# Attention and two MLPs on one core: the second head pair's transposes ahead of the first scores, a longer landing time for the gate rows in the planner, and shifted tile starts for the first MLP

## The chip, the core and the metric

The kernel runs on one core of a Trainium2 chip. Its engines are TensorE (PE; PEld is its weight load), VectorE (DVE), ScalarE (ACT), GpSimd (POOL) and SyncE (SP), which here only issues DMAs; a few DMAs are issued by ACT. The metric is the device time of one execution in microseconds. Before the change the median of three runs is 842.57 us (842.36 to 842.8). What can be told from no change here is about 0.2%, that is 1.7 us.

## The reference

For 4 batches of 8 heads (576 positions, 64 columns a head) a causal attention with a gate bias:

```python
scores = scale * np.matmul(q, k.transpose(0, 1, 3, 2))
cum = np.cumsum(np.maximum(s, 0.0), axis=-1)
scores = where(causal, -1e9, scores + min(-(cum_i - cum_j), 0))
attn = exp(scores - max) / (sum + 1e-9);  x = attn @ v
```

Then, on the 2304 tokens of 512 columns, a first MLP (512 to 1024 and back), `h = x @ w_in`, `solu = h * softmax(h)`, a layer norm with `g_ln`, `@ w_out`, and a second MLP (512 to 2048 and back) with `g = h * clip(h + 3, 0, 6) / 6`.

## The kernel before

**Two halves of an operand.** Where full precision is wanted, an operand is split into a high and a low part, and each product is three matmuls (high by high, low by high, high by low) that add up in one PSUM bank. L813 is the first product of the first MLP (weights loaded from `xh`/`xl`, `w_in_h`/`w_in_l` streamed, 128x512), L900 its second (weights loaded from `w_out`, `zh`/`zl` streamed, 128x256), L1072 and L1103 are those of the second MLP. `w_out` lies in two tiles a half: the first five chunks in one, the last `LATE_OUT` = 3 in another, which serves as score buffer first.

**Attention.** Heads go in pairs. For the first four pairs (`prep_whole`, L432) q and k are turned by PE in two groups of three transposes each (L441), and copied by ACT (q, L446) and DVE (k, L448). A score tile (`qk_whole`, L554; matmuls L584) adds two products: the gate rows (tile `whole`, rows 2 and 3) and q by k (tile `HL`, or rows 0 and 1 of `whole` from the third pair on). DVE masks and takes the row maximum (L532), ACT takes the exponential (L544), DVE the reciprocal of the row sums (L640), POOL scales (L645), PE transposes the result (L679), and L708 multiplies by v.

**Gate rows.** `gate_rows` (L266) loads `s`, sums it up on DVE, splits it (L279 to L283) and stores rows to DRAM (`rows_d`, L287); `load_gates` (L424, L428) loads each pair's rows from there into `whole`.

**The order of the work** is not that of the code. Every step is handed to a planner with an engine, a cost and the steps that it depends on; `lag` is the time that the planner allows for a DMA's landing after its issue, and `after` makes a step wait until another has begun. The planner plays the steps through with these costs, and each engine gets its instructions in that order; on the chip each engine then runs its own list from the top, waiting at each instruction until its inputs are there. The SP queue issues DMAs in the same way. So a changed cost or dependency can reorder all engines, up to where the plan comes back to the old one.

**Where tiles start.** Pools lay tiles one behind the other in each partition, so a tile's start follows from the sizes before it. Counted from a multiple of 512 bytes (128 floats, the row of one weight load), the starts are, as worked out from the pools:

| tile | L | before | with the change |
|---|---|---|---|
| xh, xl (weights) | 813 | 320 | 448 |
| w_in_h, w_in_l (streamed) | 813 | 448 | 448 |
| w_out, first five chunks (weights) | 900 | 448 | 480 |
| w_out, last three chunks (weights) | 900 | 480 | 480 |
| zh, zl (streamed) | 900 | 448 | 448 |
| x2h, x2l, w2, gh, gl | 1072, 1103 | 480 | 480 |

The tiles of the attention (`ap1`, `ap2`: whole, HL, raw q and k, y, pt, V) start 128 bytes later with the change; the second MLP's stay.

Of the kernel before, what the change touches and what calls it, by code (L numbers as in the profile page):

```python
# [10 lines left out]
F32 = mybir.dt.float32  # L11
# [177 lines left out]
def kernel(ctx, tc, q, k, v, s, w_in, w_out, g_ln, w2_in, w2_out, out):  # L189
# [5 lines left out]
    P = 128  # L195
    NH = B * H
    NPAIR = H // 2
# [38 lines left out]
    def w_out_part(late):  # L236
        for x in "hl":
            w_out_t[x, late] = w1p.tile([P, LATE_OUT if late else KFF - LATE_OUT, DM], F32R, tag=f"w_out_{x}{late:d}", name=f"w_out_{x}{late:d}")

    def w_out_at(x, c):  # L240
        late = c >= KFF - LATE_OUT
        return w_out_t[x, late][:, c - (KFF - LATE_OUT) * late, :]

    w_out_part(False)
    g_sb = w1p.tile([P, KFF], F32, name="g_sb")


    at = ExitStack()
# [6 lines left out]
        return banks[plan.bank[key]]  # L255


    mask = ap1.tile([P, 480 + P], F32, name="mask")
    nc.gpsimd.memset(mask, 0.0)
    nc.gpsimd.affine_select(out=mask[:, 480:], in_=mask[:, 480:], pattern=[[-1, P]], compare_op=ALU.is_ge, fill=NEG, base=0, channel_multiplier=1)  # L260
# [5 lines left out]
    def gate_rows():  # L266


        s_sb = ap2.tile([P, S], F32, tag="y4", name="s_sb")[:NH]
        one = ap2.tile([P, S], F32, tag="y4", name="one")[:NH]  # L270
        cum = ap2.tile([P, NQ, 2, D], F32, tag="V", name="cum").rearrange("p c j d -> p (c j d)")[:NH, :S]
        pos = ap2.tile([P, PT_COLS], F32, tag="pt", name="pos", bufs=PT).bitcast(F32R)[:NH, : 2 * S]
        neg = ap2.tile([P, PT_COLS], F32, tag="pt", name="neg", bufs=PT).bitcast(F32R)[:NH, : 2 * S]

        def load():
            nc.sync.dma_start(out=s_sb, in_=s.rearrange("b h s -> (b h) s"))

        def sums():
            nc.vector.tensor_scalar_max(s_sb, s_sb, 0.0)  # L279
            nc.vector.tensor_tensor_scan(cum, one, s_sb, 0.0, ALU.mult, ALU.add)  # L280
            nc.vector.tensor_copy(pos[:, :S], cum)
            nc.vector.tensor_sub(pos[:, S:], cum, pos[:, :S].bitcast(F32))
            nc.vector.tensor_scalar_mul(neg, pos.bitcast(F32), -1.0)  # L283

        def put(i, r, src):
            dst = rows_d[:, i, r::2, :]
            nc.sync.dma_start(out=dst, in_=src)  # L287

        def zeros(j):
            whole_t[j] = ap1.tile([P, 4, S], F32, tag=f"stack{j}", name=f"whole{j}")  # L290
            nc.gpsimd.memset(whole_t[j][:, 2:4, :], 0.0)

        plan.add("SP", 0.45, load, writes=["s"], lag=2.0)
        plan.add("POOL", 2.2, lambda: nc.gpsimd.memset(one, 1.0), writes=["one"])
        plan.add("DVE", 3.0, sums, reads=["s", "one"], writes=["c"])
        ones = one.unsqueeze(1).to_broadcast([NH, 2, S])
        both = lambda c: c.bitcast(F32).rearrange("p (i s) -> p i s", i=2)
        for i, r, src, key in ((1, 0, both(pos), "c"), (0, 1, both(neg), "c"), (0, 0, ones, "one"), (1, 1, ones, "one")):
            plan.add("SP", 0.55, lambda i=i, r=r, src=src: put(i, r, src), reads=[key], writes=[f"rows/{i}{r}"], lag=2.0)
        for j in range(2):  # L300
            plan.add("POOL", 1.3, lambda j=j: zeros(j), writes=[f"zeros{j}"], new=[(f"stack{j}", 1, f"whole{j}")])

# [251 lines left out]
    def qk_whole(p, t):  # L554

        n, w = SZ[t], ST[t] + SZ[t]
        heads = (2 * p, 2 * p + 1)
        late = ST[t] >= CUT
        ts = [i for i in range(NQ) if (ST[i] >= CUT) == late]

        def homes():
            for h, x in zip(heads, "hl"):
                if p % 2 == 0:
                    ys[h, t] = ap2.tile([P, w], F32, tag=f"y{t}", name=f"y{h}_{t}")
                elif t == ts[0]:
                    cols = sum(ST[i] + SZ[i] for i in ts)
                    if late:
                        y = w1p.tile([P, LATE_OUT, DM], F32, tag=f"w_out_{x}1", name=f"yl{h}").rearrange("p c n -> p (c n)")
                    else:
                        y = ap2.tile([P, cols], F32, tag="y2", name=f"yf{h}")  # L570
                    o = 0
                    for i in ts:
                        ys[h, i] = y[:, o : o + ST[i] + SZ[i]]
                        o += ST[i] + SZ[i]

        def mm(c0, c1, keys):
            if c0 == 0:
                homes()
            for m in range(2):
                for j in range(2):  # L580
                    r = slice(j * D, (j + 1) * D)
                    g, hl = gates_at(p, j), hls[f"HL{p}"][r]
                    a, b = (hl[:, 0, :], hl[:, 1, :]) if m else (g[:, 0, :], g[:, 1, :])
                    nc.tensor.matmul(bank(keys[j])[:n, : c1 - c0], lhsT=a[:, ST[t] : w], rhs=b[:, c0:c1], start=(m == 0), stop=(m == 1))  # L584

        pieces = pieces_of(t)
        for c0, c1, at in pieces:
            keys = [f"sc{h}_{t}_{c0}" for h in heads]
            new = []
            if c0 == 0 and p % 2 == 0:  # L590
                new = [(f"y{t}", 2, f"y{h}_{t}") for h in heads]
            elif c0 == 0 and t == ts[0]:
                new = [("wlate", 1, f"yl{p}")] if late else [("y2", 2, f"yf{h}") for h in heads]
            plan.add("PE", 4 * max(0.07, 0.00033 * (c1 - c0)), lambda c0=c0, c1=c1, keys=keys: mm(c0, c1, keys),
                     reads=[f"HL{p}/{x}{c}" for x in "qk" for c in ((0, 3) if late else (0,))] + [f"G{p}{late:d}", f"whole{p % 2}"], writes=keys, new=new, bank=keys, after=[f"sc{heads[0]}_{t}_0"] if c0 else [])
            for h, key in zip(heads, keys):
                plan.add("DVE", dve(c1 - c0), lambda h=h, c0=c0, c1=c1, at=at, key=key: tops(h, t, c0, c1, at, key), reads=[key],
                         writes=[f"{y_key(h, t)}/{c0}", f"nmax{h}_{at}"])
        for h in heads:
            exps(h, t, pieces)  # L600
# [146 lines left out]
    def pairs(a):  # L747

        r = []
        ts = [t for t in range(NQ) if (ST[t] >= CUT) == a]  # L750
        for p in range(NPAIR):
            last = (p - 1, a) if p else (NPAIR - 1, 0) if a else None
            step = [] if last is None else [(0.0, lambda last=last: norm_part((2 * last[0], 2 * last[0] + 1), bool(last[1])))]
            turns = [] if last is None else [(0.4, lambda h=h, gi=gi: tr(h, gi)) for gi in ((1, 2, 3) if last[1] else (0,)) for h in (2 * last[0], 2 * last[0] + 1)]
            extra = []
            if not a:
                if p + 1 < NPAIR:
                    extra = [(0.3, lambda p=p: prep_qk(p + 1, "q")), (0.3, lambda p=p: prep_qk(p + 1, "k"))]
                extra += [(0.0, lambda p=p: load_qk(p + 2))] if p + 2 <= NPAIR else []
                extra += [(0.0, lambda p=p: load_v(p + 1, 0))] if p + 1 < NPAIR else [(0.0, lambda: load_v(0)), (0.0, lambda: load_gates(0, 1))]  # L760
            elif p + 1 < NPAIR:
                extra = [(0.0, lambda p=p: load_gates(p + 1, 1)), (0.0, lambda p=p: load_v(p + 1))]
                if p == NPAIR - 2:
                    extra += [(0.5, lambda: prep_qk(NPAIR, "q")), (0.5, lambda: prep_qk(NPAIR, "k")), (0.0, lambda: load_qk(NPAIR + 1))]
            else:
                extra = [(0.0, lambda: load_v(NPAIR))]
            qs = [(0.0013 * (ST[t] + SZ[t]), lambda p=p, t=t: qk_whole(p, t)) for t in ts]
            k = 0
            for i, x in enumerate(qs):
                step.append(x)  # L770
                for rest in (turns, extra):
                    n = -(-len(rest) * (i + 1) // len(qs)) - -(-len(rest) * i // len(qs))
                    at = -(-len(rest) * i // len(qs))
                    step.extend(rest[at : at + n])
            if last is not None:
                step.append((1.0, lambda last=last: av(last[0], (last[1],))))
            r.append(step)
        return r
# [26 lines left out]
    def ffn1_h(i, f, kk):  # L805
        key = f"h{i}_{f}"

        def mm():
            if f == kk == 0:
                sts[i] = bcp.tile([P, 16], F32, tag="st", name=f"st{i}")  # L810
                es[i] = bcp.tile([P, 2, 512], F32, tag="e", name=f"e{i}")
            for m in range(3):
                nc.tensor.matmul(bank(key), lhsT=xs[i][m // 2][:, kk, :], rhs=(w_in_l if m == 1 else w_in_h)[:, kk, f * 512 : (f + 1) * 512],  # L813
# [162 lines left out]
    for name in "qk":  # L976
        prep_qk(0, name)
    load_qk(1)
    load_v(0, 0)
    plan.add("SP", 0.5, lambda: nc.sync.dma_start(out=g_sb, in_=g_ln.rearrange("(c p) -> p c", p=P)), writes=["g"], lag=2.0, after=["HL0/k0"])  # L980
    for b, share in enumerate(SHARES):
# [212 lines left out]
```

## Time and profile before

| | before |
|---|---|
| median of 3 runs | 842.57 us |
| the profiled execution | 840.6 us, of it 838.8 us span |
| PE busy | 810.9 us, 97% of the span |
| PEld busy | 686.1 us, 82% |
| DVE, ACT, POOL busy | 52%, 48%, 25% |
| DMA | 77.52 MB, mean 92 GB/s |

The page's first part gives busy time by engine. Views of the trace give the same by stretch (the windows), instructions in order of time (the timeline, with idle time and what ended it in brackets), groups of equal instructions (by line and form), and the chain of work that ended last. A matmul's duration runs from its start to its modelled end, and the next one starts well before that end; so a duration is compared with that of another matmul of the same shape, not added up.

### The profile page before, as it was taken

Reading aid. Unit: us, or ns where it says so; the run is one execution under the profiler, and the core shown is the slowest. Engines: PE = TensorE matmul, PEld = TensorE weight load, DVE = VectorE, ACT = ScalarE, POOL = GpSimd, SP = SyncE. Lnnn points to the kernel's source line nnn. Section 1 sums busy time; section 2 is a strip of 40 time slices with the busy share of each in tenths; the row PEclk is TensorE's granted clock in tenths of the full one; section 3 lists DMA queues with packets and bytes.
Section 4 is the critical chain, followed back from the end, with each engine's and each line's share of the span. In section 5 each row is a group of like instructions: output and inputs, shape, how many; then the busy total and the mean of one; then the engine's idle time right before and its main releaser. Section 6 shows DMA issues by size and latency. Waiting matters only on the chain.

```text
span 838.8 us, 13546 instructions
## 1 busy us (share of the span) xinstructions
PE 810.9 (97%) x4864; PEld 686.1 (82%) x4864; DVE 438.5 (52%) x1125; ACT 399.4 (48%) x928; POOL 209.9 (25%) x309
## 2 busy tenths in 40 slices
PE   3889999999999999999999999999999999999997
PEld 2555688898898889888999999998888888888886
DVE  3787887746855674739826992233222232222221
ACT  2575767755765575736635762244222322232222
POOL 2564644424632364327412220000000000000000
PEclk9999999999999999999999999999999999999999
DMA  6753596855656465323615640012000300010001
GB/s 163 194 150 112 126 214 148 175 121 125 130 119 137 99 130 121 65 95 117 198 38 192 215 152 1 0 63 89 1 0 1 101 1 0 1 51 1 0 1 50
DMA packets 95938, 77.52 MB, mean 92 GB/s; under 512 B 64288, under 2 KB 78112, under 8 KB 95872
## 3 DMA queue, kind: packets, MB, share of 16 engines
q1 hardware_dynamic: 93568, 68.27, 32.7%
q10 hardware_dynamic: 2304, 8.39, 3.0%
q8 instruction: 38, 0.62, 0.3%
q14 instruction: 28, 0.23, 0.1%
HBM read 45.38 MB, written 10.03 MB: 66 GB/s over the span
## 4 chain that ended last, share of the span: by engine, by line
PE 91%; DVE 4%; POOL 2%; DMA 2%; issue 1%; ACT 1%; POOLq 0%; DVEq 0%; SPq 0%; ACTq 0%
PE bank L1072 24%; PE bank L1103 23%; PE bank L900 11%; PE bank L813 10%; PE bank L708 6%; PE bank L679 5%; PE bank L611 5%; PE bank L584 3%; PE bank L879 2%; PE bank L474 1%; POOL y L645 1%; DVE y L532 1%; DMA stack<-HL12k 1%; DMA rows_d<-neg 1%; POOL y L627 0%
## 5 line engine op out<-in xcount | busy, mean ns | idle before, releaser
L1072 PE MATMUL bank<-x2h,w 128*128 128x512 f32 (+1 forms) x640 | 183.7, 368 | 0.0
L1103 PE MATMUL bank<-w,gh 128*128 128x512 f32 x576 | 177.0, 390 | 0.0
L1080 DVE SCALAR_TENSOR_TENSOR g<-g,bank 128x512 f32<-128x512 f32 (+1 forms) x80 | 50.7, 633 | 204.4 <-ACT g L1076 204.1
L1072 PEld LDWEIGHTS bank<-x2h,w 128*128 128x128 f32 x640 | 118.8, 188 | 17.5
L1076 ACT ACTIVATE g<-bank 128x512 f32<-128x512 f32 (+1 forms) x80 | 44.5, 556 | 178.2 <-PE bank L1072 177.9
L1103 PEld LDWEIGHTS bank<-w,gh 128*128 128x128 f32 x576 | 107.7, 188 | 21.0
L1072 PE MATMUL bank<-x2l,w 128*128 128x512 f32 (+1 forms) x320 | 117.8, 368 | 0.0
L1103 PE MATMUL bank<-w,gl 128*128 128x512 f32 x288 | 111.8, 391 | 0.0
L532 DVE CUSTOM_DVE_ANT_0 y<-bank,mask 96x288 f32<-96x288 f32 (+4 forms) x168 | 74.7, 467 | 57.4 <-PE bank L611 38.0
L544 ACT ACTIVATE y<-y,nmax 128x256 f32<-128x256 f32 (+4 forms) x140 | 83.4, 598 | 39.8 <-DVE nmax L532 27.5
L627 POOL TENSOR_SCALAR y<-y,rsum 128x128 f32<-128x128 f32 (+4 forms) x120 | 68.6, 590 | 103.8 <-DVE rsum L623 45.2
L900 PE MATMUL bank<-zh,w_out_h 128*128 128x256 f32 x288 | 82.8, 287 | 0.0
L900 PE MATMUL bank<-zl,w_out_h 128*128 128x256 f32 x288 | 81.2, 282 | 0.0
L900 PE MATMUL bank<-zh,w_out_l 128*128 128x256 f32 x288 | 81.2, 282 | 0.0
L1088 DVE TENSOR_TENSOR gl<-g,gh 128x512 fp32r<-128x512 f32 (+1 forms) x80 | 51.8, 647 | 42.2 <-ACT gh L1084 41.9
L1084 ACT CAST gh<-g 128x512 fp32r<-128x512 f32 (+1 forms) x80 | 46.2, 578 | 47.4 <-DVE g L1080 47.3
L1072 PEld LDWEIGHTS bank<-x2l,w 128*128 128x128 f32 x320 | 60.1, 188 | 7.5
L1103 PEld LDWEIGHTS bank<-w,gl 128*128 128x128 f32 x288 | 54.0, 188 | 11.3
L813 PE MATMUL bank<-w_in_h,xh 128*128 128x512 f32 x144 | 60.9, 423 | 0.8 <-DVE xh L795 0.8
L611 PE MATMUL bank<-stack 128*96 128x288 f32 (+4 forms) x288 | 57.8, 317 | 0.8 <-DMA stack<-HL12k 0.8
L813 PE MATMUL bank<-w_in_h,xl 128*128 128x512 f32 x144 | 56.9, 395 | 0.6 <-POOL xl L799 0.6
L813 PE MATMUL bank<-w_in_l,xh 128*128 128x512 f32 x144 | 56.8, 394 | 0.0
(220 smaller groups left out, 1356.4 us busy)
## 6 DMA issues: line engine op xcount, KB each, us to landing
raw_w2i<-in_moe_w_in_dram SPq DMA_DIRECT2D x16, 512.0 KB
raw_w2o<-in_moe_w_out_dram SPq DMA_DIRECT2D x16, 512.0 KB
rawq<-in_q_dram SPq DMA_DIRECT2D x32, 144.0 KB
rawk<-in_k_dram SPq DMA_DIRECT2D x32, 144.0 KB
x_d<-x2s SPq DMA_DIRECT2D x36, 128.0 KB
out_dram<-ob SPq DMA_DIRECT2D x18, 256.0 KB
raw_wi<-in_moe_w_in_dram ACTq DMA_DIRECT2D x8, 512.0 KB
raw_wo<-in_moe_w_out_dram ACTq DMA_DIRECT2D x8, 512.0 KB
```

What stands on the lines that cost most here:

```text
L532: nc.vector.tensor_tensor_reduce(out=ys[h, t][:n, c0:c1], in0=bank(key)[:n, : c1 - c0], in1=mask[:n, 480 + n - w + c0 : 480 + n - w + c1], ...
L544: nc.scalar.activation(out=y[:n], in_=y[:n], func=AF.Exp, bias=nmax[:n, h, t : t + 1], scale=-1.0, accum_out=sums[:n, h, t : t + 1])
L611: nc.tensor.matmul(bank(key)[:n, : c1 - c0], lhsT=ss[:, 2 - 2 * m, ST[t] : w], rhs=ss[:, 3 - 2 * m, c0:c1], start=(m == 0), stop=(m == 1))
L627: nc.gpsimd.tensor_scalar(ys[h, t][:n], ys[h, t][:n], rsum[:n, h, t : t + 1], 1.0, ALU.mult, ALU.mult)
L708: nc.tensor.matmul(bank(key)[j * D : (j + 1) * D, lo - c0 : c1 - c0], lhsT=vs[v_key(p, a)][:n, jj, j, :], rhs=pts[pt_key(2 * p + j, a)][:n ...
L813: nc.tensor.matmul(bank(key), lhsT=xs[i][m // 2][:, kk, :], rhs=(w_in_l if m == 1 else w_in_h)[:, kk, f * 512 : (f + 1) * 512], start=(kk ...
L900: nc.tensor.matmul(bank(key)[:, : 2 * P], lhsT=w_out_at(w, kk)[:, m * P : (m + 1) * P], rhs=z[:, kk, :], start=(kk == 0 and i == 0), stop= ...
L1072: nc.tensor.matmul(bank(key)[:, :w], lhsT=wt[:, a, 0, c * P : (c + 1) * P], rhs=x[:, c, :w], start=(c == 0 and i == 0), stop=(c == KDM - 1 ...
L1080: nc.vector.scalar_tensor_tensor(out=gg, in0=gg, scalar=6.0, in1=bank(key)[:, :w], op0=ALU.min, op1=ALU.mult)
L1084: nc.scalar.copy(gh[:, :w], gg[:, :w])
L1088: nc.vector.tensor_sub(gl[:, :w], gg[:, :w], gh[:, :w].bitcast(F32))
L1103: nc.tensor.matmul(bank(key), lhsT=g_t[ci, m][1 + i // 2][:, t * P : (t + 1) * P], rhs=w2[m][:, i % 2, 1, :], start=(m == 0 and i == 0), s ...
```

## The change

There are five edits. The turns of q and k of the second pair (`prep_qk(1, ...)`) are handed to the planner right behind the loads of that pair, and no longer among the extras of the first pair's scores; the first pair's first scores get an `after` on the last of these turns (`pp1k3`). The planner's `lag` for the stores of the gate rows goes from 2.0 to 4.5. `g_sb` (32 bytes a partition) is laid in front of the first `w_out` tiles instead of behind them; `st` of the first MLP grows from 16 to 64 floats; a tile of 32 floats that nothing uses (`apart_too`) stands in front of the mask.

```diff
+    g_sb = w1p.tile([P, KFF], F32, name="g_sb")
     w_out_part(False)
-    g_sb = w1p.tile([P, KFF], F32, name="g_sb")
...
+    ap1.tile([P, 32], F32, name="apart_too")
     mask = ap1.tile([P, 480 + P], F32, name="mask")
...
-            plan.add("SP", 0.55, lambda i=i, r=r, src=src: put(i, r, src), reads=[key], writes=[f"rows/{i}{r}"], lag=2.0)
+            plan.add("SP", 0.55, lambda i=i, r=r, src=src: put(i, r, src), reads=[key], writes=[f"rows/{i}{r}"], lag=4.5)
...
-                     reads=[f"HL{p}/{x}{c}" for x in "qk" for c in ((0, 3) if late else (0,))] + [f"G{p}{late:d}", f"whole{p % 2}"], writes=keys, new=new, bank=keys, after=[f"sc{heads[0]}_{t}_0"] if c0 else [])
+                     reads=[f"HL{p}/{x}{c}" for x in "qk" for c in ((0, 3) if late else (0,))] + [f"G{p}{late:d}", f"whole{p % 2}"], writes=keys, new=new, bank=keys, after=[f"sc{heads[0]}_{t}_0"] if c0 else ["pp1k3"] if p == 0 and not late else [])
...
-                if p + 1 < NPAIR:
+                if 0 < p < NPAIR - 1:
                     extra = [(0.3, lambda p=p: prep_qk(p + 1, "q")), (0.3, lambda p=p: prep_qk(p + 1, "k"))]
...
-                sts[i] = bcp.tile([P, 16], F32, tag="st", name=f"st{i}")
+                sts[i] = bcp.tile([P, 64], F32, tag="st", name=f"st{i}")
...
     load_qk(1)
+    for name in "qk":
+        prep_qk(1, name)
     load_v(0, 0)
```

On PE, at the start of the program, the list of before reads as follows (line, operation, what it writes and reads, its shape; the numbers are those of buffers: rawq_120 and rawk_123 belong to the first pair, rawq_148 and rawk_163 to the second):

```order
L441 MATMUL bank_97<-ident,rawq_120 128x96 x3
L441 MATMUL bank_98<-ident,rawq_120 128x96 x3
L441 MATMUL bank_99<-ident,rawk_123 128x96 x3
L441 MATMUL bank_100<-ident,rawk_123 128x96 x3
L584 MATMUL bank_101<-whole_126 128x128
L584 MATMUL bank_102<-whole_126 128x128
L584 MATMUL bank_101<-HL_138 128x128
L584 MATMUL bank_102<-HL_138 128x128
L441 MATMUL bank_103<-ident,rawq_148 128x96 x3
L441 MATMUL bank_104<-ident,rawq_148 128x96 x3
```

With the change the same place on PE reads as follows (rawq_149 and rawk_164 are the second pair's, lines are one higher):

```order
L442 MATMUL bank_97<-ident,rawq_121 128x96 x3
L442 MATMUL bank_98<-ident,rawq_121 128x96 x3
L442 MATMUL bank_99<-ident,rawk_124 128x96 x3
L442 MATMUL bank_100<-ident,rawk_124 128x96 x3
L442 MATMUL bank_101<-ident,rawq_149 128x96 x3
L442 MATMUL bank_102<-ident,rawq_149 128x96 x3
L442 MATMUL bank_103<-ident,rawk_164 128x96 x3
L442 MATMUL bank_104<-ident,rawk_164 128x96 x3
L585 MATMUL bank_97<-whole_127 128x128
L585 MATMUL bank_98<-whole_127 128x128
```

The 12 transposes of the second pair stood behind the first four and behind the first twelve score matmuls; now they stand in front of all of them, and all score matmuls of the first two pairs follow each other.

On SP, in the list of before, the loads behind the second pair's q and k stand so (whole_126 holds the first pair's gate rows, whole_135 the second's):

```order
L396 DMA rawq_148<-in_q_dram 96x6x64 x2
L396 DMA rawk_163<-in_k_dram 96x6x64 x2
L428 DMA whole_126<-rows_d 4x2x576 x2
L414 DMA V0a<-in_v_dram 128x2x64
L980 DMA g_sb<-in_moe_g_ln_dram 128x8x1
L428 DMA whole_135<-rows_d 4x2x576 x2
L396 DMA rawq_198<-in_q_dram 96x6x64 x2
```

With the change the same place on SP reads (whole_127 is the first pair's, whole_136 the second's):

```order
L397 DMA rawq_149<-in_q_dram 96x6x64 x2
L397 DMA rawk_164<-in_k_dram 96x6x64 x2
L415 DMA V0a<-in_v_dram 128x2x64
L983 DMA g_sb<-in_moe_g_ln_dram 128x8x1
L429 DMA whole_127<-rows_d 4x2x576 x2
L429 DMA whole_136<-rows_d 4x2x576 x2
L415 DMA V0a<-in_v_dram 128x2x64
```

A load of v (V0a) and that of g_sb now stand ahead of the first pair's gate rows, and the second pair's gate rows directly behind them.

On PE, at the place where the first product of the first MLP begins, the list of before reads (rawq_355 is the fifth pair's q):

```order
L474 MATMUL bank_97<-ident,rawq_355 128x96 x3
L474 MATMUL bank_99<-ident,rawq_355 128x96 x3
L813 MATMUL bank_102<-w_in_h,xh_556 128x512
L813 MATMUL bank_102<-w_in_l,xh_556 128x512
L813 MATMUL bank_102<-w_in_h,xl_557 128x512
```

And with the change (rawk_382 is the fifth pair's k, whole_136 serves the fourth pair's scores here):

```order
L475 MATMUL bank_100<-ident,rawk_382 128x96 x3
L585 MATMUL bank_103<-whole_136 96x480
L585 MATMUL bank_99<-whole_136 96x480
L585 MATMUL bank_103<-whole_136 96x480
L585 MATMUL bank_99<-whole_136 96x480
L814 MATMUL bank_97<-w_in_h,xh_570 128x512
L814 MATMUL bank_97<-w_in_l,xh_570 128x512
L814 MATMUL bank_97<-w_in_h,xl_571 128x512
```

Score matmuls and the turns of the fifth pair's k, which stood behind the first of these products, now stand ahead of them. The lists of all engines differ in many places up to about a fifth of PE's list, and are the same from there on.

## Rows read from the trace of the kernel before

**Rows 1.** The page, busy us (share of the 838.8 us span) and instructions.
```profile
PE 810.9 (97%) x4864; PEld 686.1 (82%) x4864; DVE 438.5 (52%) x1125; ACT 399.4 (48%) x928; POOL 209.9 (25%) x309
```
**Rows 2.** Windows: stretch, length, busy us of each engine, granted clock, DMA share, GB/s.
```profile
32.00:64.00 32.00, 28.14 (x190) 18.57 (x190) 25.00 (x80) 21.44 (x56) 19.27 (x23) 1.00 0.59 158
64.00:100.00 36.00, 34.21 (x230) 20.42 (x229) 28.55 (x84) 23.16 (x58) 19.96 (x27) 1.00 0.49 120
```
**Rows 3.** Chain that ended last, up to 33 us: start, us, what.
```profile
8.61 4.26 DMA rows_d<-neg
13.02 2.40 DMA whole<-rows_d
...
17.10 1.15 PE bank L441 x6
...
20.26 0.69 PE bank L441 x3
...
24.86 2.04 DMA rawq<-in_q_dram
...
27.83 2.90 PE bank L584 x16
```
**Rows 4.** Timeline of SP's DMA issues: start, us, line, what.
```profile
10.21 1.74 SPq L396 DMA_DIRECT2D rawk<-in_k_dram  x2
13.02 0.60 SPq L428 DMA_DIRECT2D whole<-rows_d  x2
13.66 0.41 SPq L414 DMA_DIRECT2D V0a<-in_v_dram  x1
14.13 0.46 SPq L980 DMA_DIRECT2D g_sb<-in_moe_g_ln_dram  x1
```
**Rows 5.** Timeline of PE: start, us, line, what [idle before <-releaser].
```profile
15.56 0.90 PE L584 MATMUL bank<-whole 64*128 64x128 f32 x3 [8.22 <-DMA whole<-rows_d]
...
22.25 0.60 PE L584 MATMUL bank<-HL 64*128 64x256 f32 x4
23.89 0.69 PE L441 MATMUL bank<-ident,rawq 96*128 96x96 f32 x6 [1.04 <-DMA whole<-rows_d]
...
26.02 0.55 PE L679 MATMUL bank<-ident,y 128*128 128x128 f32 x3 [0.98 <-POOL y L645]
...
36.56 1.80 PE L584 MATMUL bank<-whole 64*128 64x128 f32 x16
...
53.96 0.50 PE L813 MATMUL bank<-w_in_h,xh 128*128 128x512 f32 x1 [0.80 <-DVE xh L795]
...
55.32 0.50 PE L813 MATMUL bank<-w_in_h,xl 128*128 128x512 f32 x1 [0.63 <-POOL xl L799]
```
**Rows 6.** Timeline of POOL, the first normalisation.
```profile
24.29 2.55 POOL L645 TENSOR_SCALAR y<-y,rsum 128x128 f32<-128x128 f32 x4 [0.77 <-DVE rsum L641]
```
**Rows 7.** Groups by line and form, whole span: count, busy us, mean ns of one.
```profile
L813 PE MATMUL bank<-w_in_h,xl 128*128 128x512 f32 x144 | 56.9, 395 | 0.6 <-POOL xl L799 0.6
```
**Rows 8.** The same groups within 440 to 560 us.
```profile
L1103 PE MATMUL bank<-w,gh 128*128 128x512 f32 x166 | 51.3, 392 | 0.0
L1103 PE MATMUL bank<-w,gl 128*128 128x512 f32 x83 | 32.5, 395 | 0.0
```
**Rows 9.** The same groups within 560 to 838.8 us.
```profile
L1103 PE MATMUL bank<-w,gl 128*128 128x512 f32 x205 | 79.3, 389 | 0.0
```
**Rows 10.** Timeline of PE, within one group of 24 matmuls of L900.
```profile
329.75 0.28 PE L900 MATMUL bank<-zh,w_out_l 128*128 128x256 f32 x1
...
331.43 0.28 PE L900 MATMUL bank<-zh,w_out_h 128*128 128x256 f32 x1
...
332.37 0.28 PE L900 MATMUL bank<-zl,w_out_h 128*128 128x256 f32 x1
```
**Rows 11.** Windows on PE: stretch, length, busy us, granted clock, DMA share, GB/s.
```profile
27.90:31.40 3.50, 3.50 (x20) 0.51 0.70 213
```
**Rows 12.** Waits on PE between 60 and 440 us.
```profile
PE bank L708 <- DVE pt4b L683: 1.8, 1, 1.8
```

## The prediction

> **What bounds the kernel now.** I read the busy times first: PE is busy for 810.9 of 838.8 us [rows 1], so the kernel is a line of PE instructions, and time goes where PE idles or where its matmuls come further apart. The windows then tell where it idles: nearly all before 100 us. Of the 32 us from 32 to 64, PE is busy for 28.14, of the next 36 for 34.21 [rows 2]; no other engine is full there (DVE 25.00 and 28.55, POOL 19.27 and 19.96). The timeline of PE shows the largest hole, 8.22 us up to 15.56, in which it has turned the first pair's q and k and waits for the gate rows [rows 5]. The chain shows why: the store of the negated rows takes 4.26 us to land, and the load back, issued at 13.02, another 2.40 [rows 3]. Behind 15.56 the chain runs over the second pair's turns (six transposes in 1.15 us, the last three in 0.69), whose place is between the scores [rows 3]. Then come waits of 1.04 us (the third pair's q) and 0.98 us (POOL's normalisation) [rows 5]. Last, the groups by line and form tell how dense the matmuls are.
>
> **The turns in front of the first scores.** This moves work into the hole and takes 1.15 + 0.69 = 1.84 us off PE's line [rows 3]. What is late next is the start of the scores itself. First, the k turns need the second pair's k, issued in two halves from 10.21 on, the second at about 11.0 [rows 4]. No row has its landing; the nearest are 2.04 us in a quiet stretch and 4.26 us in this crowded one [rows 3], so 13.0 to 15.3, and up to 16.2 counted from the end of the issue at 11.95. I take 15.7, near the crowded row; six transposes at 1.15 end at 16.9. So the wait that was hidden behind the gate rows is now about level with them. Behind the waiting turns stand all scores on PE, and nothing else can pass.
>
> **The longer landing in the plan.** It puts a load of v and that of `g_sb` ahead of the first gate rows on SP. The issue costs nothing: 11.95 + 0.41 + 0.46 = 12.82, before 13.02, when the rows could be issued anyway [rows 4]. But their transfers (64 KB, and 1024 pieces of 4 bytes) now lie ahead of the gate rows'. Their price is not shown: nothing if they run beside each other, 2.40 if they cost a landing of their own [rows 3]. I take 1.4, above the middle, since all three were issued on one queue: 15.42 + 1.4 = 16.8. Both reasons agree on a start of the scores at 17.0 in place of 15.56: +1.45.
>
> **Up to the third pair's scores.** The first two pairs' scores ended at 22.25 + 0.60 = 22.85 [rows 5] and now end at 22.85 + 1.45 - 1.84 = 22.45. The wait of 1.04 goes: the third pair's q can be issued when the second's is turned, near 16, and at 2.04 to 4.26 us is there before 22.45. What is late then is POOL: its four normalisations ran from 24.29 for 2.55 us, to 26.84 [rows 6]. DVE's decoding of `w_in`, which stood between the maxima ahead of them, moves partly into the hole, and one more pair's maxima stand ahead; I let POOL start 0.5 earlier and end at 26.3. The last transposes (0.44) end at 26.75, the turns of k that stood behind them are already done, and the third pair's scores start at 26.75 in place of 27.83 [rows 3]: **-1.1**. With the start at 15.56 it is -2.5, with a full 2.40 for the loads ahead about -0.1.
>
> **The clock.** From 27.9 to 31.4 the granted clock was 0.51, the level of 1.2 GHz, after a stretch in which PE had waited 1.04 and 0.98 us [rows 5, 11]. Sixteen score matmuls took 2.90 us there; the sixteen from 36.56 on, at the upper level, took 1.80 [rows 3, 5]. With shorter waits the fall may not come: -1.1. PE still waits for POOL, so I leave this out of the sum and in the range.
>
> **Up to 100 us.** Ahead of the first product of the first MLP PE waited 0.80 (DVE) and 0.63 us (POOL) [rows 5]. Four score matmuls and the turns of the fifth pair's k (0.69 for half of them when PE is slow) now stand ahead of it. They hide 0 to 1.43; I take **-0.7**, as POOL's wait may come up elsewhere.
>
> **The tile starts.** L813's matmuls take 395 ns [rows 7]; their weights start at 320, the streamed operand at 448 (the table of starts). L1103, of the same shape with all starts at 480, takes 389 in the second MLP's later part, but 392 and 395, mean 393, where it alternates with narrower matmuls [rows 8, 9]. With equal starts L813 can gain 6 ns on each of 3 x 144 = 432 matmuls, 2.6 us, or 2 ns, 0.9 us, or nothing (the 395). L813 comes in short runs among other work, so the mixed stretch is nearest: **-1.0**. In L900 the five chunks with w_out and z at the same start are 120.0 ns apart (14 steps in 1.68 us), the three with starts 32 bytes apart 117.5 (8 steps in 0.94 us) [rows 10]. All chunks now have the second relation: 2.5 ns on 36 x 5 x 3 = 540 matmuls is 1.35 us, at least nothing; a loss is excluded, since the three chunks show this very pair of starts. I take half, **-0.7**. Scores and L708 have both operands in tiles that move together: nothing. The transposes read `ident`, which stays, and tiles that move by 128 bytes; no row shows it. At L900's 2.5 ns, 32 heads of 15 blocks and 16 pairs of 12 are 672 transposes, 1.7 us either way, costed at nothing.
>
> Here a rule speaks against the change. In the Trainium skill, TensorE: Matmul & The Clock Gate, section Step-by-step: what each phase is for, weight load and streamed operand have independent read ports, so that the one takes no bandwidth from the other. By that, tile starts would give nothing, and the sum would be 1.7 us less. That L900's chunks differ with their starts is against it; that L1103 with the same starts differs by up to 6 ns between two stretches is for something else than starts.
>
> **Sum.** -1.1 - 0.7 - 1.0 - 0.7 = -3.5 against the profiled execution's 840.6: 837.1. The median of the runs stands 1.97 above that execution, so the forecast is 842.57 - 3.5 = 839.1.
>
> **Rivals.**
> Starts count for nothing, and only the order helps: 842.57 - 1.8 = 840.8. For it: runs of L813 are short. Chance 0.20, half of it within 0.2% (1.7 us), which is what a measurement can tell.
> The order gives nothing (gate rows a full 2.40 later, the waits before 64 us come up elsewhere), starts give 1.7: 840.9. For it: DMA runs at 0.59 and more there [rows 2]. Chance 0.15, half of it within 0.2%.
> Slower: the seam between attention and first MLP. PE has spent on earlier places the scores and turns that filled its time there, and arrives before POOL, which has to normalise and to form low halves. The waits of 0.80, 0.63 and 1.8 us stand there already [rows 5, 12]; if two of them grow by a set of four normalisations (2.55 [rows 6]), that is +5.1, against -1.1 and -1.7: 844.9. It decides once new waits between 32 and 100 us exceed 2.8 + 1.7 = 4.5 us. Against it: POOL is idle for 12.7 of 32 us. Chance 0.12.
> More: the clock stays up (-1.1) and L813 reaches 389 ns (another -1.6): 836.4. Chance 0.13.
> Forecast: 0.40, a tenth of it within 0.2%.
>
> So faster 0.36 + 0.13 + 0.10 + 0.07 = 0.66, same 0.04 + 0.10 + 0.08 = 0.22, slower 0.12. The range, 835.9 to 842.8, takes in the better case and stops short of the slower one.
>
> **What would show it.** In the profile after: the second pair's turns between 13 and 17; the first scores at 17.0 (15.6 says that the loads ahead are free, 18 that they cost a landing); the third pair's scores near 26.7; no granted clock of 0.5 behind 27.9 if the better case holds; less than 3 us of idle PE from 32 to 64; L813 at 392 to 393 ns (389: all of the 2.6; 395: starts are nothing); L900 a nanosecond or two denser from start to start. The prediction is wrong if PE's idle time between 32 and 100 us grows, or if the transposes' durations move.

## The result, and the profile after: slower by 1.2%

| | before | after |
|---|---|---|
| median of 4 runs each, same chip | 842.47 us | 852.73 us |
| ratio, 95% interval | | 1.0121 (1.0108 to 1.0134) |
| profiled execution, its span | 840.6, 838.8 us | 852.6, 850.8 us |
| PE idle, its timeline's holes added up | 23.7 us | 29.9 us |
| stretches at granted clock 0.50, without one in the last 2 us of each span | 3.4 us | 17.1 us |

The forecast was 839.1 us, faster. The kernel is 10 us slower, outside the range. The last two rows of the table give the account: 6.2 us more idle, and 13.7 us more at the 1.2 GHz level, which counted at half are 6.8 us. Together they are 13.0; the spans differ by 12.0, and the 1 us that is left the other way is about what the tile starts give (e1 below). The medians differ by 10.3 only, because the profiled execution of before is 1.9 us faster than its median.

Where it is lost, the windows tell (those of before are [rows 2]; the first line here is before, the others are after; columns as there):

```profile
100.00:150.00 50.00, 49.22 (x375) 41.46 (x374) 41.32 (x136) 37.27 (x98) 23.91 (x37) 1.00 0.79 176
```
```profile
32.00:64.00 32.00, 28.06 (x156) 16.97 (x157) 21.06 (x67) 15.39 (x41) 11.28 (x15) 0.89 0.45 124
64.00:100.00 36.00, 33.71 (x208) 22.04 (x207) 27.66 (x77) 22.21 (x53) 20.26 (x26) 0.95 0.43 116
100.00:150.00 50.00, 44.79 (x319) 36.76 (x318) 37.75 (x120) 33.28 (x86) 19.89 (x30) 0.93 0.62 146
```

PE gets through 34, 22 and 56 fewer instructions in the same times: the loss lies before 150 us, while PE's busy time as a whole (page of after) is larger than in [rows 1], since the half clock stretches it:

```profile
PE 816.8 (96%) x4864; PEld 690.8 (81%) x4864; DVE 441.9 (52%) x1125; ACT 399.8 (47%) x928; POOL 207.0 (24%) x309
```

The 41st of L813's 144 products of three matmuls starts at 195.1 us before and at 207.9 after, the last one at 414.3 and 426.5, so behind that the distance no longer grows.

PE's timeline of after, the rows with more than 1 us of idle time ahead of them and those that the forecast spoke of (compare [rows 5]):

```profile
14.37 1.19 PE L442 MATMUL bank<-ident,rawq 96*128 96x96 f32 x6 [7.27 <-DMA rawq<-in_q_dram]
...
16.61 0.80 PE L585 MATMUL bank<-whole 64*128 64x128 f32 x4
...
23.49 0.69 PE L442 MATMUL bank<-ident,rawk 96*128 96x96 f32 x6 [1.60 <-DMA rawk<-in_k_dram]
...
25.11 1.58 PE L585 MATMUL bank<-whole 64*128 64x128 f32 x16
...
33.05 1.07 PE L585 MATMUL bank<-whole 64*96 64x480 f32 x3 [4.10 <-DMA whole<-rows_d]
...
43.97 1.79 PE L585 MATMUL bank<-whole 64*128 64x384 f32 x4 [2.18 <-DVE a_wi L333]
...
67.06 0.27 PE L680 MATMUL bank<-ident,y 96*128 96x96 f32 x1 [1.27 <-DVE HL4q L487]
...
120.94 0.76 PE L612 MATMUL bank<-stack 128*96 128x288 f32 x2 [4.83 <-DMA stack<-HL5k]
```

The head came out better than forecast: first scores at 16.61, right behind the last turn (forecast 17.0), third pair's scores at 25.11 (26.75; before 27.83). On SP the loads that the plan put ahead of the gate rows cost 0.6 us of issue (compare [rows 4]), and POOL is done at 24.69 (compare [rows 6]):

```profile
12.10 0.92 SPq L415 DMA_DIRECT2D V0a<-in_v_dram  x1
13.07 0.46 SPq L983 DMA_DIRECT2D g_sb<-in_moe_g_ln_dram  x1
13.64 1.46 SPq L429 DMA_DIRECT2D whole<-rows_d  x4
```
```profile
22.82 1.87 POOL L646 TENSOR_SCALAR y<-y,rsum 128x128 f32<-128x128 f32 x4 [8.66 <-DVE rsum L642]
```

Then come three new long waits, 11.1 us together; waits of before that are gone or shorter make up for 4.9 of them. The first only takes back what the head had gained: the scores behind it start at 33.05, and in the kernel before they start at 33.08:

```profile
33.08 1.13 PE L584 MATMUL bank<-whole 64*96 64x480 f32 x4
```

So the 12 us come behind 33 us. With the first and the second wait, and inside the third, the granted clock falls (windows at PEclk 0.50; one more fall follows waits of 1.27 and 0.33 us at 66 us):

```profile
33.90:37.30 3.40, 3.40 (x12) 1.41 (x9) 0.73 (x3) 0.79 (x2) 0.00 (x0) 0.50 0.25 57
44.20:47.50 3.30, 3.30 (x11) 2.22 (x11) 3.27 (x15) 0.34 (x1) 2.37 (x4) 0.50 0.49 160
68.10:71.40 3.30, 3.30 (x16) 2.89 (x15) 2.39 (x5) 1.87 (x3) 3.30 (x5) 0.50 0.32 111
119.30:126.00 6.70, 5.07 (x18) 4.41 (x19) 1.19 (x3) 0.22 (x1) 0.66 (x1) 0.50 0.71 151
```

The chain of after tells what ended the first wait. The gate rows were not late in their transfer; they were issued at 30.90, and what came before that on the chain is a weight load of ACT (start, us, what):

```profile
26.02 4.82 DMA raw_wi<-in_moe_w_in_dram
...
30.90 2.02 DMA whole<-rows_d
...
33.05 3.47 PE bank L585 x7
```

Why a load on SP follows a load on ACT, the built program tells. All DMAs of SP and ACT take eight completion semaphores in turn, in the order in which the program lists them, and a DMA waits until the one eight places ahead of it, which had the same semaphore, has landed. The trace bears this out: it has 400 such DMAs, 50 on each of eight semaphores in this turn, and SP's wait for the semaphore of raw_wi3 ends at 30.84 us. In the list of after:

```
30  ACT  raw_wi3, 512 KB              semaphore 6
31, 32  SP  gate rows, fourth pair    7, 0
33      SP  second half of V1a        1
34-37   SP  fourth pair's q and k     2, 3, 4, 5
38      SP  gate rows, first pair     6   stands until 30 has landed
39  ACT  raw_wi0, 512 KB              7
```

In the list of before, ACT's weight loads stand at 22, 30, 38 and 46: each follows the last at a distance of eight and waits for nothing but its forerunner. Of 16 weight loads six have another weight load eight places behind them before, counted by the semaphores in the trace (e8's expectation says 7); after, none has. The view of waits for SP's queue (0 to 200 us; line waited for: us, times, longest) puts a number on it, first before, then after:

```profile
SPq L416 <- DMA raw_wo<-in_moe_w_out_dram: 2.6, 1, 2.6
```
```profile
SPq L397 <- DMA raw_wo<-in_moe_w_out_dram: 7.2, 2, 4.3
SPq L429 <- DMA raw_wi<-in_moe_w_in_dram: 5.5, 2, 5.2
SPq L397 <- DMA raw_wi<-in_moe_w_in_dram: 3.2, 1, 3.2
```

SP stands behind weight loads for 15.9 us in place of 2.6 (2.9 with a 0.3 not shown). Not all of that is loss: the buffer of the gate rows was read until 26.7, so of the 5.2 us at 30.9 some 4 count.

The second wait is of another kind. Its gate rows wait for no weight load: SP issues them when the scores that read their buffer have ended, and by the semaphore in the trace they land at 43.83 (the view names a DVE instruction, which ends within 0.1 us of that):

```profile
40.58 0.61 SPq L429 DMA_DIRECT2D whole<-rows_d  x2
```

Whether a shared semaphore costs the time, or PE's new order by itself, had to be tried.

### The profile page after: what moved, and what is told of

It reads as the page before. It is cut to its first block, busy times and chain, and to the rows that moved or that the text cites. A ratio compares the mean times of both kernels' runs of the same rounds, so it can differ in the third digit from the quotient of the medians.

```text
span 850.8 us, 13565 instructions
## 1 busy us (share of the span) xinstructions
PE 816.8 (96%) x4864; PEld 690.8 (81%) x4864; DVE 441.9 (52%) x1125; ACT 399.8 (47%) x928; POOL 207.0 (24%) x309
## 4 chain that ended last, share of the span: by engine, by line
PE 87%; DVE 5%; DMA 3%; POOL 2%; issue 1%; ACT 1%; SPq 0%; POOLq 0%; DVEq 0%; ACTq 0%
PE bank L1075 23%; PE bank L1106 23%; PE bank L901 12%; PE bank L814 10%; PE bank L709 5%; PE bank L612 5%; PE bank L680 5%; PE bank L585 2%; PE bank L880 2%; PE bank L475 1%; POOL y L646 1%; DMA stack<-HL5k 1%; DMA raw_wi<-in_moe_w_in_dram 1%; DMA rawq<-in_q_dram 1%; DVE y L533 0%
## 5 line engine op out<-in xcount | busy, mean ns | idle before, releaser
L545 ACT ACTIVATE y<-y,nmax 128x128 f32<-128x128 f32 (+4 forms) x140 | 83.4, 597 | 34.9 <-DVE nmax L533 28.3
```

The lines of the kernel that those rows point to most:

```text
L545: nc.scalar.activation(out=y[:n], in_=y[:n], func=AF.Exp, bias=nmax[:n, h, t : t + 1], scale=-1.0, accum_out=sums[:n, h, t : t + 1])
```

## The experiments

Idle time, half clock and the time that SP stood behind weight loads come from the profiled execution of each; the ratio is to before, on the same chip. The span is 813 us + idle + half of the half-clock time, within 1.1 us for all of these but e4 and e10 (2.9 and 1.8 us under it). SP held, alone, does not order the times: it counts every load that stands behind a weight load, also those that PE does not wait for.

| run | time, us | ratio (95%) | idle | half clock | SP held | span |
|---|---|---|---|---|---|---|
| before | 842.1 to 842.9 | 1 | 23.7 | 3.4 | 2.9 | 838.8 |
| after | 852.73 | 1.0121 (1.0108 to 1.0134) | 29.9 | 17.1 | 15.9 | 850.8 |
| e1 starts alone | 841.01 | 0.9983 (0.9973 to 0.9993) | 24.3 | 3.4 | 4.9 | 839.2 |
| e2 order alone | 853.99 | 1.0132 (1.0113 to 1.0152) | 32.5 | 13.6 | 16.7 | 852.8 |
| e3 turns alone | 852.03 | 1.0119 (1.0094 to 1.0145) | 30.0 | 10.2 | 10.9 | 848.9 |
| e4 lag alone | 860.35 | 1.0212 (1.0195 to 1.0229) | 37.5 | 20.5 | 15.2 | 857.9 |
| e5 a tiny load between | 846.27 | 1.0038 (1.0020 to 1.0056) | 26.3 | 10.2 | 8.9 | 844.6 |
| e6 the same, elsewhere | 841.11 | 0.9982 (0.9972 to 0.9992) | 23.3 | 6.8 | 3.6 | 840.0 |
| e7 after, loads by POOL | 847.33 | 1.0065 (1.0040 to 1.0090) | 26.3 | 10.2 | 0 | 845.3 |
| e8 e1, loads by POOL | 850.29 | 1.0087 (1.0068 to 1.0106) | 29.5 | 13.6 | 0 | 848.5 |
| e9 after, aligned | 845.14 | 1.0030 (1.0018 to 1.0043) | 25.0 | 10.2 | 11.4 | 843.5 |
| e10 gate landing 3.5 | 850.81 | 1.0089 (1.0058 to 1.0120) | 31.6 | 17.1 | 16.8 | 851.4 |
| e11 last loads by POOL | 851.69 | 1.0107 (1.0086 to 1.0127) | 30.1 | 17.1 | 11.8 | 850.6 |
| e12 e9, less on DVE | 843.60 | 1.0019 (1.0007 to 1.0031) | 24.1 | 6.8 | 11.1 | 841.5 |

**e1 to e4: the change in its parts.** e1 is before with the three tile edits, e2 before with the two others, e3 with `prep_qk(1, ...)` and its `after` alone, e4 with `lag=4.5` alone (their lines are those of the diff above).

> The three tile starts alone (g_sb in front of w_out, st of 64 floats, the unused tile of 32 floats); order of before. Theory A (the loss of 10 us comes with the new order: a gate-row load that stands on SP until a 512 KB weight load of ACT has landed, a load of HL5k that comes late at 116 us, and the half granted clock behind each of these waits): 839.5 to 841.3, that is 1.2 to 3 us under before, L814 at a spacing of about 227 ns in its long runs in place of 232. Rival B (the shifted starts are what costs, in transposes or copies): 850 or more. Rival C (starts give and cost nothing): 842.5.

> The order alone (turns of the second pair in front, lag 4.5), tile starts of before. Theory A: 853.5 to 856, with the waits of 4.10 us at 29 us and 4.83 us at 116 us as in the full change, and the granted clock at 0.5 for some 17 us behind them. Rival B (starts cost): about 842. Rival C: 852.7, as the full change.

> The turns in front alone, lag 2.0 as before. In its list the gate-row load for the first pair's second half no longer waits for the semaphore that the 512 KB load raw_wi3 uses (row 33 of SP waits for another), while PE's order is nearly that of the full change. Theory A: the wait of 4.10 us at 29 us and the half clock behind it go, so 4 to 7 us less than the order alone: 847 to 850, with the wait at 116 us still there if SP's list around HL5k is the changed one. Rival D (it is PE's order itself, scores spent too early, whatever the semaphores): 853 to 856, the same waits within 1 us.

> The longer landing in the plan alone, turns where they were. The gate-row load of row 33 on SP waits for another semaphore than raw_wi3's here too; two 512 KB loads stand closer together on ACT. Theory A: no wait of 4 us at 29 us; what is left are the start of the scores (+0 to 1.5 us) and what the changed list does at 116 us: 843 to 849. Rival D (PE's order with the turns in front is the cause): 841 to 844, since the turns stand where they stood. If the lag alone brings the loss: 852 or more.

e1 and e2 came in time as theory A has them: the starts give 1.4 us (0.17% of 842, interval 0.6 to 2.3), and the order alone costs 11, though in e2 the wait at 116 us is 6.41 in place of 4.83 and the half clock 13.6 us in place of 17. e3 and e4 did not. The turns alone cost 10 us, the longer landing alone 18, both together 11: each gives another plan, and the prices do not add up. In e3 the wait at 29 us fell to 2.22 us as expected, since there the weight loads stand eight apart in that stretch, but it did not go, since the gate rows, issued at 27.25, took 4.64 us to land; the second wait is 2.55 us and that at 113 us still 4.91: 852 in place of 847 to 850. In e4 I had looked at one row of SP only; there it is the second half of k, just ahead of the gate rows, that stands behind raw_wi3, for 6.8 of the 7.57 us of this row (its two halves):

```profile
25.82 7.57 SPq L396 DMA_DIRECT2D rawk<-in_k_dram  x2
```

PE waits 4.79 us behind it, and then 6.61 us at 64 and 5.75 at 104 us. These two long waits of e4 were not followed to their cause, nor why e3 costs nearly as much as e2, with the first wait only about half as long (2.22 and 4.16).

**e5 and e6: the good order, spoilt by 4 bytes.** To e1 one load is added on SP, `nc.sync.dma_start(out=apart_too[:1, :1], in_=g_ln.rearrange("(c p) -> p c", p=P)[:1, :1])`, in `load_qk` ahead of one q: the fourth pair's (e5), the seventh's (e6).

> Order and starts of e1_starts (841.0), and one more load of 4 bytes on SP, just ahead of the fourth pair's q. In the built program all DMAs of SP and ACT take eight completion semaphores in turn, and a DMA waits until the one eight places ahead of it has landed. With the extra load the DMA eight places behind ACT's 512 KB raw_wi3 is no longer ACT's next weight load but the second half of the fourth pair's k on SP, with the gate rows behind it. Theory L (these shared semaphores are what costs): SP stands at that half of k until raw_wi3 has landed at about 31 to 32 us, the gate rows are issued at about 32.5 in place of 29.5, PE waits 2 to 3 us ahead of its 128x480 scores near 33 us, the granted clock falls once more behind it: 843.5 to 846.5. Rival D (the loss comes from PE's order in the plan, not from semaphores): 840.5 to 841.8, since a load of 4 bytes is all that is added.

> The control for e5: the same load of 4 bytes on SP in the kernel with the starts alone (841.0), but ahead of the seventh pair's q near 100 us, where no weight load of ACT stands within the eight places ahead of it, so that every weight load keeps the DMA that stood eight places behind it. Theory L: 840 to 842, SP held by weight loads for under 4 us in all. Rival (a small extra load on SP is itself what costs): 844 or more.

Both came in time as theory L has them: e5 is 5.3 us over e1, e6 0.1. PE's work and its order are the same in all three, so this pair shows that one load of SP behind a weight load can cost this much. SP's timeline, the chain and PE's timeline of e5, and behind them the rows of e1 in the same place (SP, PE):

```profile
24.24 0.24 SPq L396 DMA_DIRECT2D apart_too<-in_moe_g_ln_dram  x1
25.31 0.88 SPq L399 DMA_DIRECT2D rawq<-in_q_dram  x2
26.24 0.49 SPq L417 DMA_DIRECT2D V1a<-in_v_dram  x1
27.61 6.06 SPq L399 DMA_DIRECT2D rawk<-in_k_dram  x2
33.78 0.71 SPq L431 DMA_DIRECT2D whole<-rows_d  x2
```
```profile
27.87 5.47 DMA raw_wi<-in_moe_w_in_dram
...
33.78 2.88 DMA whole<-rows_d
```
```profile
36.79 2.19 PE L587 MATMUL bank<-whole 64*96 64x480 f32 x4 [4.97 <-DMA whole<-rows_d]
```
```profile
29.49 0.61 SPq L429 DMA_DIRECT2D whole<-rows_d  x2
```
```profile
32.77 1.23 PE L585 MATMUL bank<-whole 64*96 64x480 f32 x4 [0.25 <-DMA whole<-rows_d]
```

The load of 4 bytes takes 0.24 us on SP. It moves the second half of the fourth pair's k into the place eight behind raw_wi3, SP stands there (5.4 of the 6.06 us of that row), the gate rows are issued at 33.78 in place of 29.49 (e1), and PE waits 4.97 us in place of 0.25, twice what I had expected. The half clock that goes with it (6.8 us) is part of the price. Two of the ten executions of e5 took 842.1 and 842.2 us, the others 844.9 to 849.2: the price is not paid each time, and only one execution has a trace.

**e7 to e9: the changed order, mended.** In e7 and e8 `issue = nc.sync if behind is None else nc.scalar` names `nc.gpsimd` at its end: POOL issues the weight loads, with semaphores of its own. In e9 two loads of v go to POOL, `(nc.gpsimd if (key, j) in (("V1a", 1), ("V4", 1)) else nc.sync)`.

> The full change, with the 512 KB weight loads issued by POOL in place of ACT, which takes other semaphores, so no DMA of SP waits for a weight load. Theory L: the waits of 4.10 us (29 us) and 4.83 us (116 us) shrink to 0 to 2.5 us each and most of the half-clock stretches go: 840 to 845, unless POOL's issuing costs more than 0.3 us a load on the way of its normalisations (16 loads; then up to 3 us more, read off e8). Rival D: both waits stay within 1 us: 851 to 854.

> Order and starts of e1_starts (841.0) with the weight loads issued by POOL, as the control for e7. Theory L: in this order 7 of 16 weight loads are followed eight places on by another weight load of ACT and hold up no load of SP, so little is to be gained: 840 to 843, what POOL's issuing costs. If it is 844 or more, POOL's issuing itself costs and e7 is read against this.

> The full change (852.7) with two loads of v that nobody waits for yet (second half of V1a, second half of V4's first part) issued by POOL in place of SP. Each takes one DMA out of the turn of eight semaphores, so that eight places behind raw_wi3 stands ACT's raw_wi0 and eight behind raw_wo5 ACT's raw_wo6, as in the order of before. Theory L: the gate rows are issued at 26 to 27.5 us in place of 30.9, PE's wait at 29 us falls from 4.10 to 0.5 to 2.2 us, that at 116 us from 4.83 to under 2, at least one of the four half-clock stretches goes: 843 to 848. Rival D: no change, 851 to 854.

e9 came in time as theory L has it: two loads that nobody waits for leave the turn, and 7.6 of the 10.3 us are back. The gate rows are issued at 28.56, and PE reaches their scores without a wait (timelines of SP and of PE; the second PE row is the wait that was 2.18):

```profile
28.56 0.60 SPq L429 DMA_DIRECT2D whole<-rows_d  x2
```
```profile
31.34 1.15 PE L585 MATMUL bank<-whole 64*96 64x480 f32 x4
...
40.36 1.19 PE L585 MATMUL bank<-whole 64*128 64x384 f32 x4 [2.17 <-DMA whole<-rows_d]
```

The gate rows are later than expected (26 to 27.5), since the scores read their buffer until then. No run takes two loads from SP without changing what stands behind the weight loads, so what that alone gives is not separated. The wait at 116 us, of which I had given theory L most, fell only from 4.83 to 3.56, with DVE as its releaser.

e7 and e8 both missed: 847.33 in place of 840 to 845, and 850.29 in place of 840 to 843. e8 says that POOL's issuing is dear in itself (9.3 us over e1), and why I can't tell from one run; against it e7 is 3.0 us faster, so with no load of SP held, the changed order was not the worse one. In e7 the wait at 29 us is gone, the second is 0.69, but the third still stands, with no load of SP held anywhere (timelines of SP and of PE):

```profile
111.42 0.46 SPq L493 DMA_DIRECT2D stack<-HL5q  x1
111.94 1.44 SPq L494 DMA_DIRECT2D stack<-HL5q  x1
113.42 0.60 SPq L493 DMA_DIRECT2D stack<-HL5k  x1
114.18 0.74 SPq L494 DMA_DIRECT2D stack<-HL5k  x1
```
```profile
116.03 0.48 PE L612 MATMUL bank<-stack 128*96 128x288 f32 x2 [3.92 <-DMA stack<-HL5k]
```

These loads go into a buffer that PE reads until 111.39, and are issued from 111.42 on. So of the 4.83 us at 116 the shared semaphores bring about 0.9, by this comparison; the rest goes with the order. A new wait of 4.90 us at 58 (DVE, HL4q) is part of why e7 missed.

**e10 and e11: a better version sought, and not found.** e10 has the turns in front, the starts, `lag=2.0` for the stores, `lag=3.5` in `load_gates`, and three loads of 4 bytes ahead of V4's second; e11 leaves these three out and issues wo5 to wo7 by POOL.

> A search for a better version: turns in front and tile starts as in the full change, lag of the stores 2.0, landing of the gate rows' loads in the plan 3.5 in place of 2.0 (the trace has 2.0 to 4.6), and three loads of 4 bytes ahead of the second load of V4, which put ACT's raw_wo6 eight places behind its raw_wo5. Theory L with the plan's landing as second cause: the waits of 2.2 us at 30 and 39 us go, SP is held by weight loads for under 9 us: 838 to 844. If PE's order with the turns in front is worse in itself (DVE's chain ahead of the scores at 111 us stays): 844 to 848.

> As e10_gates (850.8), without the three small loads, and with the last three weight loads (raw_wo5 to raw_wo7) issued by POOL, so that from 90 us on no load of SP can stand behind a weight load. In e10 PE's idle time up to 100 us and its clock were better than before's, and all was lost in one wait of 6.58 us at 114 us, where a load of HL5q stood 4.7 us behind raw_wo6, and in 10.2 us at half clock behind it. Theory L: that wait falls to 1 to 3.6 us (what is left is DVE's chain) and half clock behind it to 0 to 7 us: 838.5 to 845. Rival D (PE's order is the cause of the wait at 114 us): 849 to 852.

e10 missed (838 to 844 expected, and SP held under 9 us; 16.8 were measured). Up to 92 us it did what was wanted: the waits at 31 and 37 us are 0.53 and 0.59, and no half clock stands before 92 us. Then SP stood 4.7 us behind raw_wo6 with a load of HL5q, and PE 6.58 us at 114 us. In e11 that wait is 2.92, as theory L expected, but the time is not: 1.96 and 0.82 us came up at 136 and 140 us, in a chain that runs over the weight load that POOL issued late (128.38, 7.20 us), and the half clock stayed at 17.1 us. The expectation of 838.5 to 845 was wrong, since it took one wait away and counted on nothing behind it; the same mistake as in the forecast.

**e12: what is left in e9.**

> e9_aligned (845.1) with DVE's decoding of two chunks of w_out left out (the low bits t_wo and the join into a_wo of wo4 and wo5, four instructions; what these two chunks hold is then not the reference's). In e9 PE waits 3.56 us at 111 us for DVE's row maxima, ahead of which DVE works through the join of wo4 (0.68 us at 104.25) and the decoding of wo5 (0.42 and 0.88 us at 112.13). Theory D' (what is left of the loss is that PE's order asks at 111 us for maxima that DVE, full there, cannot give yet): the wait falls by 1.3 to 2 us, and the half clock of 3.4 us that begins in it may go: 841.5 to 844. Rival (the wait is for the loads of HL5q and HL5k, DVE is only named): the wait stays within 0.5 us, 844.5 to 846.

The time lies in the range of theory D', the wait between the two. DVE had its maxima 2.03 us after PE had come to wait, in place of 3.31, but the wait fell by 0.70 only, and now ends with a DMA (PE's timeline of e12):

```profile
112.69 0.48 PE L616 MATMUL bank<-stack 128*96 128x288 f32 x2 [2.86 <-DMA stack<-HL5k]
```

So two things come late there, within 0.9 us of each other: DVE's maxima and a load into a buffer whose last reader has just finished. The median fell by 1.5 us, but on another chip; by the ratios to before it is 0.9, and the two intervals overlap, so the gain is not shown. The stretch of half clock that is gone (3.4 us) is not the one in this wait but that at 63 us.

## Why the prediction was wrong, point by point

Two steps failed, "The longer landing in the plan" and "Up to 100 us". The first costed SP's new order by the time of its issues and by transfers that lie ahead at the head, and said that the issue costs nothing. At the head that did no harm: the gate rows were issued 0.6 us later, and were there when the turns had ended. It did not hold behind: a DMA on SP can wait for one of ACT's, and which for which depends on the count of DMAs between them. Moving a few loads shifts this count all through the attention; the turns in front shift it too (e3), so the same holds for that edit. I compared the lists by what stands in a row, never by what a row waits for, where it can be read. "Up to 100 us" let the waits of before shrink by 0.7 and gave new ones no term; they are 11.1 us by 121 us, with four falls of the clock.

How much of this the semaphores bring is shown in part. The first wait (4.10 us) is theirs for the most part: it is gone in e9 and e7, and e5 makes such a wait in the good order; in e3, where no weight load holds its gate rows, 2.22 us are left, since they land late. The second (2.18) is not: its gate rows stand behind no weight load, and e9 has 2.17 there. They took up to 3.3 us from issue to landing in after and in e9, and 1.9 in e7, where the wait is 0.69; in after and e9 a 512 KB load was issued 1.4 to 1.5 us ahead of them, in e7 none in the 4 us ahead. That would fit, but was not tried. Most of the third (4.83) is not theirs either (3.92 in e7). So for these two the forecast missed that PE, with its scores in another order, comes back to a buffer before it can be filled again.

- **The turns in front, and up to the third pair's scores**: the mechanism was right, the size too small. Third pair's scores 2.7 us earlier in place of 1.1; POOL's normalisations ran from 22.82 in place of 23.8 as forecast. The wait of 1.04 us for the third pair's q went, but one of 1.60 for its k came at 23.49. All of the gain is given back in the wait at 29 us: the buffer of the gate rows is read until 26.7 and filled again from 30.90.
- **The clock**: the fall at 27.94 went, as the better case had it, and four others came. I had counted the clock only as a gain. Counted at half, it doubled the price of the waits here: 6.2 us more idle time came with 13.7 us more at half clock, that is 6.8.
- **The starts**: -1.7 forecast, -1.4 measured (0.6 to 2.3), and e6, on another chip, has the same ratio as e1. In the traces L900's part is seen in uninterrupted runs of two groups of 24 matmuls, from the first row to the row behind the run: before 5.71 us, e1 5.68:

```profile
390.67 0.28 PE L900 MATMUL bank<-zh,w_out_h 128*128 128x256 f32 x1
...
396.38 0.60 PE L879 MATMUL bank<-ident,e 128*128 128x128 f32 x4
```
```profile
391.30 0.28 PE L901 MATMUL bank<-zh,w_out_h 128*128 128x256 f32 x1
...
396.98 0.60 PE L880 MATMUL bank<-ident,e 128*128 128x128 f32 x4
```

  Times 18 that is 0.5 us (0.7 forecast; each time is rounded to 0.01, so 0.2 to 0.9). L813 gave less than its 1.0: from start to start 232 ns become 227 (medians) behind 360 us, where its runs are long, and stay at 232 to 233 in the mixed stretch, some 0.5 us in all. Together these are about 1 us of the 1.4. The mean of L813's row went from 395 [rows 7] to 394 in e1, not to the 392 to 393 that was to show the gain; the steps from start to start show it better. L813 gained with its two operands at equal starts, L900 with starts 32 bytes apart, so no rule on starts follows. The Trainium skill (TensorE: Matmul & The Clock Gate, Step-by-step: what each phase is for) gives weights and streamed operand read ports of their own. Read as in the prediction, that starts then give nothing, it is against e1's interval; the page itself says nothing of tile starts.
- **The rivals**: "slower" was there with 844.9, at the seam, by POOL. The side was right; the place, the mechanism and the size (2.3 us slower in place of 10.3) were not. POOL releases none of the three new waits.
- **The signs named**: PE's idle time from 32 to 100 us grew, from 5.65 to 6.23 us by the windows, as the sign of a wrong prediction had it; by far the larger loss there is the clock. The transposes' durations did not move (275 and 246 ns in e1 as before), so costing them at nothing was right.

What stays open, beside e4 and e8: why the order of after, aligned, is still 4.1 us over e1 (e9 to e1). Idle time is only 0.7 of it; 3.4 are two more stretches of half clock, behind 1.28 us of waiting at 61 us and within the 3.56 at 111. Why these fall and before's waits of 1.79 us at 92 and of 0.80 and 0.63 at 53 [rows 5, 12] don't, no run here tells. Weight loads on ACT with semaphores of their own were not tried.

The version that beats both is e1: the tile starts without the new order, 841.01 us, 0.17% under before.

## What to carry to other kernels

When a change reorders DMAs, read for every load on the path what it waits for, the completion semaphore that it shares included, and look whether a long transfer of another queue stands just so many places ahead; an urgent small load behind a 512 KB one stood there 5.4 us (e5). A plan that is good may be so by such an alignment, which no line of code shows, and a load of 4 bytes can undo it. Do not put every new wait down to the first cause found: here one of three was this, and the other two came for the most part from buffers that PE asked for too early. A gain at the head is worth what the next buffer's refilling leaves of it, and a wait is to be priced with the fall of the clock that may come with it.

## What the runs showed of the hardware

The clock was the larger part of a wait's price: e5 has 2.0 us more idle time than e1 and 6.8 us more at half clock, 3.4 of the 5.4 us of span. POOL's issue of a weight load takes 0.53 to 0.77 us in the trace of e8, and yet e8 lost 9.3 us by 16 of them. The 128x256 matmuls of L900 stand 118.9 ns from start to start (5.71 us for 48) with five of eight chunks at the same tile start as the streamed operand, 118.3 with all eight 32 bytes away from it (e1); the 128x512 matmuls of L813, in long runs, 232 ns with starts 128 bytes apart and 227 with equal ones.
